# One order of issue replaced by another: the same 2916 pieces of DeltaNet attention and Fourier mixing, and 54 unread products on TensorE in place of 20

## The chip, the cores and the metric

The kernel runs on one core of a Trainium2 chip. The metric is the device time of one launch in microseconds (us). Five engines work from queues of their own, each in its own order: TensorE (PE, with its weight loads shown as PEld), VectorE (DVE), ScalarE (ACT), GpSimd (POOL) and SyncE (SP), which issues the DMAs. Everything is in float32.

## The reference

What must be computed, cut to what matters:

```
q, k, v: (4, 8, 768, 48)   beta: (4, 8, 768)   w_ch1: (384, 1536)   w_ch2: (1536, 384)

# attention (DeltaNet), for each batch and head, t = 0 .. 767
k_n   = k / (norm(k) + 1e-6);  state = 0                     # state is 48 x 48
y[t]  = q[t] @ state
state = state + beta[t] * outer(k_n[t], v[t] - state.T @ k_n[t])

x = y in the layout (batch, 768, 8 * 48 = 384)

# mixing, for each batch
u   = x + real(fft over the 384 channels of (fft over the 768 positions of x))
un  = (u - mean(u)) / sqrt(var(u) + 1e-6)                    # over the 384 channels
out = u + relu(un @ w_ch1) @ w_ch2
```

## The kernel before

**Attention.** The 768 positions of a batch are cut into six units (u0 to u5 for batch 0) of 128 positions, all 8 heads together. In a unit, the recurrence becomes products of 64x64 blocks and the inverse of a triangular matrix. Units are worked in rounds. The first round holds u0 and u1, the second u2 to u5, and both are prepared at once at the start of the kernel, which is called the **front** here. Its steps, with the names that the trace shows:

- `turn` transposes the keys on PE by products with a unit matrix (the helper line L358); ACT or DVE copies the result out of PSUM (L364 is a copy on ACT, L366 and L368 one on DVE).
- `keys` multiplies the transposed keys with each other (PE, 64x64 products; every ordinary matmul has the helper's line L355).
- `begin16` and `invert16` invert the 16x16 diagonal blocks on DVE, all heads at once, in pairs of a multiplication (L772) and an addition (L778) whose length changes from step to step. The steps of the two rounds alternate. Then come a scaling (L791) and two block transposes (L801 and L797).
- `join` puts the 16x16 inverses together to 32x32: DVE adds two of them (L832, into the tile `lo`), PE multiplies (`pp<-lo,w`), ACT copies the product back to `lo`, PE multiplies again (`pp<-lo,us`), and DVE subtracts the result in four pieces (L878) and transposes (L886, L887). After that come the 64x64 blocks, and the chain over the units.

Between these run the copies of `scale_v` (eight ACT copies of 128x48, `us<-us,nr`) and the decoding of weights (`f0` is L2019 and `f2` L2025 on ACT, then steps on DVE and POOL up to L2038).

**Mixing.** When a batch's attention is done, `seq6` does the transform over positions, and `feat` the one over channels: for each of six tiles T0 to T5 of 128 positions, PE writes two PSUM banks (`pp<-ft,R`), ACT copies the second of them to `ss`, and DVE adds and subtracts the first against it (L1530, L1533) and adds to `x` (L1537). `normed` normalises and `blockwise` transposes (L1591); a DMA through `zd` brings the transposed tile back as `R`. The MLP then runs in groups g0 to g2 of two tiles. For the last batch it is `mlpw`: a form with fewer products, in which DVE first adds and subtracts inputs (L1791) and weights (L1765), PE runs `first_w` (`pp<-R,w`, `pp<-us`, `pp<-us,w`, `pp<-R,us`) and `second`, and DVE takes the sums out of PSUM (L1962). The attention of batches 1 to 3 runs between the mixing of the batches before. The last batch's mixing, from about 512 us on, has no attention left beside it; this is called the **tail** here.

**What sets the order.** The program doesn't issue what it computes directly. `Plan.op` records 2916 pieces (one piece is what one engine does at one go: some matmuls, a copy, a DMA). `Plan.issue` then reads the text ORDER, 78 lines of signs, and issues the pieces in its order on all engines at once: two signs name a piece, one more the engine where a piece may run on one of several, one the PSUM bank for each bank that it opens, and two the piece after which a paced DMA may go. A number past the last piece calls `fill`:

```
            i = take(2)
            if i >= len(self.ops):
                fill(i - len(self.ops), take(1))
                continue
```

`fill(kind, bank)` issues products of the constant tile `pack` into a PSUM bank; nobody reads them. Kind 4 is one product of 128x128 by 128x256, which the trace shows as two passes under L2241; kind 3 is two products of 64x64 by 64x256 side by side; kind 0 is 18 small ones (L2235). A fill takes its place in PE's order as any other product, and it waits until what stood in its bank has been read out. Each engine works strictly in the order of ORDER, so that order also decides what stands behind a waiting instruction.

Of the kernel before, what the change touches and what calls it, by code (L numbers as in the profile page):

```python
# [62 lines left out]
CvDGtoAGrAnDeCDfDDgCiDjDiDhC0CHDCPGqCWDkDlDJABBXDmDKCGdC5CBGfC6CsDpAB1GeGgB4B5DqDoCBjC-DEDtCDrCDuCDs
CDnCCyB8B9CACBCECFCIASGyGyGlGzGfHCCTBZDACJDvFDwDxCDyCCMBkDLGHCNCQCRCUCVCYCZCcD0CCdCjBlDzCD3ABD5CCkD4
CClD1CDD6ED2CD8CDEOD7CFQEAECCEDCEBFAEEDHDdD9CEFCHMD+BCD-CEJEGETDG0CmEQCEKCFRCERBELCEUESCEPCEVCCnGnGo
EMEWDEXEYC7CVMKB1G6ETHEFUCENCEwEZEaEbEcEdFSCGpFTBEICEzCFVCFWDMG7CQGhEyCEfCGsGtFXCEHBEgDEhEkCElCEuFGE
vBDNCnFYAFZHfEYEiCEjCHOEeCDTELEmHHNEnFbFcDOBDQBHcEHHTHTFaEoCFdFeFfE2MmHEEpCErCDRBHPGuEqCG8G1E4BFhBEs
BCExAHDWDWE0FiGEtCHSHSE1CGvGwHQG3E5E+BCG2G4E7CE6BE8E3CE-CHeGhHGFjHdEfDPBFgCE9BGxG9FCFECHFHHHIFFCHVHP
FDDAFGFHBFlCFnCFmCFABCFLHUFZFkBFoHFNBFBBFpMnENHgHiHhFIMaEoFrCFMBHjHkFsCFJBNLFqCFOFPBHJFtCFuFGFKCDSE9
FyHWF0BMNGvMMFcFwBCIAE7FvCFzFHHRF1CHYF2MoGDG-HXG+HAMqCFxBH+FwF3BF7F9CF8CMLE6F4F5CHZHaHlF6BF+H0H0GACD  # L70
F-CGEMpCJNHyF9GBCGGCGCBCGHCHbMPF2GFGHH-G-GIIBF8GDCJMG5JOJPGKGJCMbMbHBHpFsJRJQGNGOBJTMcFDHoG+GMCH9GGH
8MpJSGLCGPCGQJVMdCJUJWJZGRCMeCJcMrABGUGWCGSCDDUFDJXMfEFGVCMtCGTBGXJYJaJbJeJfJiMOGPJdJgJjMgH1FNGYCHzF
zMhCJhHrGMJkGZCICJlJnJmJrDVG5JpJuHGH2MkCMwCMvCMjCH4H3MsJoJqHnFxJsHqJZMiCMuCH5H6JvJ3DCJ4HmMgJtMlJwQVM
hHsHtQ6MwHvHuHwH7MxJ1BJ5MyJMMRGOJxCJzCJ7CMzG5JyCJ0BIDM0EFJ9CJ6CHxKAABJ2CKJHDMQJoM2CM1BKBJ8CKDM-J7KSG
FKCJ-CJ+BKEKbCEKKKLKMIFKFKNIUJ5KTKcIEIGM+MiKGKkAEKUKVNABFKOKHKIKeNCCQXH2NBCIJIJKPKQM3GHKdIWJ1IVM0K2K
RKlK5KtFDKuK3BIHKWKXKYK6CIXM2INHsIIJkILJtNDDEIKJ0K4CK7CNJK8CIMHuQWJcM7CQiKlM6BIfKtIjK6KZIYKnNICM9NHC
KaKfKvKgKwQhKVRFM6IOIPNEQ5MeNFCM5BQRKTLHBM8CIeK6IiKSIgJ0NGCIQK+FIaIRISKhLRIZM4LSK9CIbIcQSNHLBDIhJ8Ki
NKLICLEEITNMK-CNNNONPIvKkIkIuNDIdNQNRNZNaNbNcNdLCCQjFGIsKKQlCQ7CHKjImLULFCIqIqLKBNeNfQ8CNgIlNhNiInIo
RGM3IrKYI5LHNjKmI4NGItKWIpNkI2NKLVJCQ8QkCNlNmQ9CNnNoNpNqNrNsNtQ+GHREQmDEQYKvQnIwIxIzKoLAFAI3QjZeLLCN
# [36 lines left out]
6e9BimBlTe+ilCXreLeMeNlUlVfAlWfCfDBjVi8Cffe-lXioFijDEeOfECfceTi+ABikCfBipfgeJjWFiqDEisCjDBlYlZlalbir
fJhYBjXCjCCitDjBClcldleeCi-EFivABiujYDfFjACjEEFeDfGfIfHiyfMjGBjZBXPjFePlflgfLjbCjcCfKjaClhlifNfOfQfR
fSfUljlkfhfafoDfTfXixCfpCllfiEjHDfjCfPizfWlmfVfqjdFCjeGHfrftjIjiCfkiwBjJDEflfmjhClnloeEjfCfsfnfuAHBl
plqfvCjKgegfClrfwCjgCf1jLClsjMDjyltlumPBmOBlvCeFgajOFEjNjjCDjzj0ktClwClxf2GjkjlClyDXtmQgbCjSjRmRElzB
j-lmjmCmSBf3CfzjnfxjQmTGfyf4f5f7mWBf0l0El1BjoCDgcmXBjPjqCf8f6l3BgDmVCjpl2BmUBj2l4Cl5GEmuCmtCmvkuBl9B  # L120
l8Cl+CggjrFjsl6DCl7Bf9Gf+Bl-CDmwFmxCmYGEmAmBCmCFmbCmcCmDf-mZCDmdCmEFGgAgEEj3maCmGBmFgFCghlwmHDgBj1mJ
CFj4mIgCgImyGm0BmeDEgGgHgJgKgLmgCmzCmMmfmNmKmLmhFm2CmijtCDm1BmjEFmkn9jugMgOgTgNgPkvBgQgRgSmlCgUgXn+g
VnKgdgdgijpn-oAnSGnUEnTBgWgYm3FAnVCm4HGjwm7CjvmmBnWmnoBoEm6CmoCEoCm5Cm9GHnLmqoDnbBm+mpmsncCoFmrnAFoH
nBoGoIoJnYm-CoKneCm8CnfCnXnCEFnECnZoNoMnaBGACoLnDnFHFoOngninhnjnInJjxnHnGoQoPoRoSoUoToWndnknlFnmCoXo
VnoHoYoZoagZnpCobocEDodnqokHFofCoeBnMnrohBojCj5oiBolomCopCo2EDo3oqBo4osFDoto5o6ovouo7o8owooBoxoyozo0
pAEDnnnNnto9orBnsonBo1poppBnupqnwproHo+ogCpBo-psptBpupDpCpEpFpKHFpLpNpMpOpUDFnOpPnynvpQpGnPnQn0pHpIp
# [2148 lines left out]
```

## Time and profile before

| What | Value |
| --- | --- |
| three runs | 628.64, 631.59, 635.98 us; median 631.59 |
| profiled execution | 629.09 us, of which the span of its instructions is 627.3 |
| mean granted TensorE clock in it | 0.985 |
| PE busy | 598.4 us (95% of the span) |
| DVE, ACT, POOL busy | 532.2 us (85%), 308.1 us (49%), 30.6 us (5%) |
| instructions | 22553 |
| moved by DMA | 40.65 MB, mean 65 GB/s |

The profile shows, for one execution, the busy time of each engine, the same in 40 slices of the span, the chain of work that ended last, and groups of instructions. PEclk is the TensorE clock that was granted, as a share of full speed. A PE row of the timeline joins matmuls of one kind that follow each other without a gap, and says in brackets how long PE was idle before and what ended that. A float32 matmul appears as two passes, except a transpose.

### The profile page before, as it was taken

The numbers are of one execution on the slowest core, as the hardware profiler recorded it, in microseconds if no ns is written. First come the engines' busy times: TensorE is split into PE (matmuls) and PEld (weight loads), VectorE is DVE, ScalarE is ACT, GpSimd is POOL, SyncE is SP. The second block draws the span as 40 slices with busy tenths as digits, with TensorE's granted clock in tenths as the row PEclk, the third lists the DMA queues.
The fourth block names the chain that finished last, engine by engine and source line by source line (L and its number), as shares of the span: only waits on it lengthen the run. The fifth ranks groups of instructions, "written<-read, shape, count | busy, mean of one in ns | idle before, by whom it ended". The sixth has DMA issues, their size and how long they took to land.

```text
span 627.3 us, 22553 instructions
## 1 busy us (share of the span) xinstructions
PE 598.4 (95%) x9674; PEld 520.5 (83%) x9674; DVE 532.2 (85%) x1460; ACT 308.1 (49%) x851; POOL 30.6 (5%) x39
## 2 busy tenths in 40 slices
PE   7789899989999989999999999999999998899997
PEld 6668798857778768799898878799989897899997
DVE  5978899999999879999889999998988987677464
ACT  5779777654447554856453256473433216233120
POOL 2001511230000000000000000000000000000000
PEclk9889999999999999999999999999999999799999
DMA  8625365432132421213113120503001001020101
GB/s 179 197 61 136 107 168 128 128 100 39 27 79 43 92 58 37 58 35 102 30 28 77 28 40 1 128 1 102 16 28 29 28 1 51 3 100 26 51 0 52
DMA packets 100578, 40.65 MB, mean 65 GB/s; under 512 B 88316, under 2 KB 95965, under 8 KB 100477
## 3 DMA queue, kind: packets, MB, share of 16 engines
q1 hardware_dynamic: 100285, 38.97, 24.3%
q8 instruction: 76, 1.25, 0.8%
q10 hardware_dynamic: 192, 0.23, 0.1%
q14 instruction: 25, 0.20, 0.1%
HBM read 30.14 MB, written 9.04 MB: 62 GB/s over the span
## 4 chain that ended last, share of the span: by engine, by line
PE 78%; DVE 12%; ACT 5%; issue 2%; DMA 1%; POOL 0%; DVEq 0%; SPq 0%; ACTq 0%; POOLq 0%
PE pp L355 75%; ACT us L364 2%; PE pp L358 2%; PE pp L2241 1%; DVE R L1377 1%; DVE x L1962 1%; DVE us L607 1%; DVE w L2038 1%; DVE pm L1377 1%; ACT R L364 1%; PE pp L2235 1%; DMA us<-in_q_dram 1%; DVE x L1352 1%; DVE u L1292 1%; DMA R<-in_k_dram 1%
## 5 line engine op out<-in xcount | busy, mean ns | idle before, releaser
L355 PE MATMUL pp<-R,w 128*128 128x256 f32 (+1 forms) x832 | 181.1, 368 | 0.0
L355 PEld LDWEIGHTS pp<-R,w 128*128 128x128 f32 x832 | 145.9, 192 | 18.7 <-issue 0.5
L355 PE MATMUL pp<-us 64*64 64x64 f32 (+6 forms) x2704 | 92.0, 236 | 12.0 <-ACT us L364 9.3
L355 PEld LDWEIGHTS pp<-us 64*64 64x64 f32 (+3 forms) x2704 | 76.9, 137 | 20.2 <-ACT us L364 12.9
L355 PE MATMUL pp<-w,R 128*128 128x384 f32 (+1 forms) x288 | 91.3, 441 | 1.8 <-DVE w L2038 1.8
L364 ACT ACTIVATE us<-pp 32x128 f32<-32x128 f32 (+4 forms) x149 | 57.9, 404 | 63.8 <-PE pp L355 39.3
L355 PEld LDWEIGHTS pp<-w,R 128*128 128x128 f32 x288 | 51.9, 190 | 24.4 <-DVE w L2038 2.4
L964 DVE TENSOR_TENSOR rr<-rr,tmp 128x30 f32<-128x30 f32 (+10 forms) x150 | 51.0, 340 | 3.1
L959 DVE TENSOR_TENSOR tmp<-rr 128x30 f32<-128x30 f32 (+10 forms) x150 | 48.9, 327 | 3.3
L1858 DVE TENSOR_TENSOR us<-us,pp 128x256 f32<-128x256 f32 x64 | 26.0, 419 | 18.5 <-ACT us L364 12.4
L355 PE MATMUL pp<-u,us 64*48 64x48 f32 (+2 forms) x1360 | 39.4, 216 | 0.2
L355 PEld LDWEIGHTS pp<-u,us 64*64 64x64 f32 (+1 forms) x1360 | 33.9, 130 | 5.8 <-issue 3.2
L1893 ACT ACTIVATE R<-pp 128x512 f32<-128x512 f32 x20 | 12.0, 598 | 40.0 <-PE pp L355 36.0
L364 ACT ACTIVATE gd<-pp 32x256 f32<-32x256 f32 x65 | 23.8, 374 | 15.4 <-PE pp L355 4.8
L355 PE MATMUL pp<-ft,R 97*128 97x97 f32 (+1 forms) x192 | 26.4, 283 | 4.6 <-DVE x L1962 3.7
L364 ACT ACTIVATE x<-pp 64x384 f32<-64x384 f32 (+2 forms) x39 | 17.0, 440 | 27.7 <-PE pp L355 13.3
L364 ACT ACTIVATE u<-pp 64x192 f32<-64x192 f32 (+1 forms) x65 | 21.2, 326 | 18.4 <-PE pp L355 10.8
L355 PEld LDWEIGHTS pp<-ft,R 97*128 97x128 f32 (+1 forms) x192 | 23.8, 193 | 6.6 <-DVE x L1962 3.8
L355 PE MATMUL pp<-R,ws 128*128 128x192 f32 x144 | 28.6, 329 | 0.1
L355 PE MATMUL pp<-us,gd 128*128 128x192 f32 x144 | 27.6, 326 | 0.0
L355 PE MATMUL pp<-st,us 48*64 48x48 f32 (+1 forms) x1104 | 25.7, 221 | 1.0 <-DVE u L366 0.5
L364 ACT ACTIVATE us<-us,nr 128x48 f32<-128x48 f32 x104 | 24.6, 322 | 2.4 <-DMA us<-in_v_dram 2.4
(217 smaller groups left out, 1082.9 us busy)
## 6 DMA issues: line engine op xcount, KB each, us to landing
R<-zd SPq DMA_DIRECT2D x44, 96.0 KB
out_dram<-x SPq DMA_DIRECT2D x11, 384.0 KB
us<-in_k_dram SPq DMA_DIRECT2D x16, 192.0 KB
us<-in_q_dram SPq DMA_DIRECT2D x16, 192.0 KB
us<-in_v_dram SPq DMA_DIRECT2D x16, 192.0 KB
x<-in_moe_w_ch_dram SPq DMA_DIRECT2D x11, 242.0 KB
zd<-tv SPq DMA_DIRECT2D x11, 192.0 KB
zd<-pm SPq DMA_DIRECT2D x11, 192.0 KB
```

Source lines behind the costliest of these rows:

```text
L355: I(nc.tensor.matmul(o, lhsT=lhsT, rhs=rhs, start=start, stop=stop, skip_group_check=True))
L358: I(nc.tensor.matmul(o, lhsT=src, rhs=ident[p0:p0 + n, p0:p0 + n], is_transpose=True, start=start, stop=True, skip_group_check=True))
L364: I(nc.scalar.activation(o, i, ACT.Copy, **({} if scale is None else {"scale": scale})))
L607: I(nc.vector.tensor_tensor(z.LT.rearrange(hs, s=2), span(b, 0, 128, [[64, NJ], [1, 64]]), m_su[:, None, None, :].broadcast_to([128, 2, NJ ...
L959: I(eng(e).tensor_tensor(T_, R[:, :, j + 1:32, j:j + 1].broadcast_to([128, ns, n, j]), R[:, :, j:j + 1, 0:j].broadcast_to([128, ns, n, j]) ...
L964: I(eng(e).tensor_tensor(R[:, :, j + 1:32, 0:j], R[:, :, j + 1:32, 0:j], T_, op=ALU.add))
L1292: I(nc.vector.tensor_tensor(U, U, span(b1, 64 * c, 64 * c + 64, [[D, m], [1, D]], s0), op=ALU.subtract))
L1352: I(nc.vector.tensor_tensor(w, w, v, op=ALU.add))
L1377: I(eng(e).tensor_tensor(o, i0, i1, op=op))
L1858: vec(256, lambda e: I(nc.vector.tensor_tensor(o, i0(), i1(), op=ALU.add)), [], [aH] + list(wr), pr - P.ev, use=n)
L1893: I(nc.scalar.activation(o, s, ACT.Relu))
L1962: vec(n, lambda e: I(nc.vector.tensor_tensor(o(), i0(), i1(), op=op)), rd, wr, pr - P.ev, use=use, due=due)
```

## The change

Only the text ORDER is replaced, by one that is a line longer, so that every line of the code below it has a number higher by one (L358 becomes L359, L2241 becomes L2242). The first line of each:

```diff
-ANBAPDAODALDAAADBAEDAMDAGDAHDACDAWAQDtkFAZANAYAaAHAbHAA6ANAXATABAKBAcCAeCBA7ANAdBAhFGAgBAfCAiAIDA4AN
+AMBAFDAYAAAPBAJDAWAEBACBtkAAZAPAKBAaAKAHDABAbFAAdBAIBAeGBAcCAhCDAgBAfCAiAUAAODAjATA6APBJHFA5AKA4A4A-
```

The 2916 pieces and their code are the same. What differs is their order on every engine; the engine of 190 pieces (91 go from DVE to ACT, 90 from ACT to DVE, 7 from POOL to DVE, 2 from DVE to POOL); the PSUM bank of nearly all; the piece that paces most DMAs; and the fills, of which there are 54 now (50 of kind 4, three of kind 3, one of kind 0) and were 20 (17, 2 and 1). They lie here:

| Place in the program | fills before | fills now |
| --- | --- | --- |
| front, up to the chain over u0 | 13, and kind 0 once | 34, and kind 0 once |
| later in the chain of batch 0 | 0 | 1 |
| middle, about 200 to 260 us | 6 | 8 |
| tail, between the `feat` tiles and ahead of the first `first_w` | 0 | 10 |

Two places in full; a row is a run of like instructions. First PE in the front, from the middle of the transposes to the second product of `join`. `us` here are keys, 128x64 rows are transposes, the 64x64 rows on `us` alone are `keys`, and `lo_74` is the tile `lo` of the first round. Before:

```order
L2241 MATMUL pp<-pack 128x256 x3
L358 MATMUL pp<-pack,us 128x64 x16
L2241 MATMUL pp<-pack 128x256 x3
L358 MATMUL pp<-pack,us 128x64 x24
L355 MATMUL pp<-us 64x64 x48
L355 MATMUL pp<-lo_74,w_65 64x64 x16
L2241 MATMUL pp<-pack 128x256
L355 MATMUL pp<-lo_74,us 64x64 x16
```

and with the change:

```order
L2242 MATMUL pp<-pack 128x256 x4
L359 MATMUL pp<-pack,us 128x64 x8
L2242 MATMUL pp<-pack 128x256 x3
L359 MATMUL pp<-pack,us 128x64 x8
L356 MATMUL pp<-us 64x64 x16
L359 MATMUL pp<-pack,us 128x64 x8
L2242 MATMUL pp<-pack 128x256 x2
L356 MATMUL pp<-us 64x64 x16
L2242 MATMUL pp<-pack 128x256 x2
L356 MATMUL pp<-us 64x64 x16
L356 MATMUL pp<-lo_74,w_65 64x64 x16
L2242 MATMUL pp<-pack 128x256
```

Fills now stand between single transposes and between the products of `keys`, up to the first product of `join`; before, none stood between the last transposes and `join`. (Ten more fills stand ahead of these rows now, seven of them in one row, where seven stood in one place before.)

On DVE at the same place, the last steps of `invert16` ahead of the addition L832 of the first round. Before:

```order
L772 TENSOR_TENSOR tmp<-w_66 128x52 x2
L778 TENSOR_TENSOR w_66<-w_66,tmp 128x2x13x2
L778 TENSOR_TENSOR w_66<-w_66,tmp 128x2x2x13
L772 TENSOR_TENSOR tmp<-w_66 128x72
L772 TENSOR_TENSOR tmp<-w_66 128x28
L778 TENSOR_TENSOR w_66<-w_66,tmp 128x2x12x3
L778 TENSOR_TENSOR w_66<-w_66,tmp 128x2x14
L791 TENSOR_TENSOR w_66<-w_66,gb 128x16x16 x2
L801 STREAM_TRANSPOSE rr<-w_66 128x16x32
L797 STREAM_TRANSPOSE gd<-w_66 128x16x32
L832 TENSOR_TENSOR lo_74<-gd,rr 128x128
```

and with the change:

```order
L773 TENSOR_TENSOR tmp<-w_66 128x52 x2
L779 TENSOR_TENSOR w_66<-w_66,tmp 128x2x2x13
L773 TENSOR_TENSOR tmp<-w_66 128x28
L753 STREAM_TRANSPOSE nr<-nr 128x32
L779 TENSOR_TENSOR w_66<-w_66,tmp 128x2x14
L792 TENSOR_TENSOR w_66<-w_66,gb 128x16x16 x2
L802 STREAM_TRANSPOSE rr<-w_66 128x16x32
L798 STREAM_TRANSPOSE gd<-w_66 128x16x32
L833 TENSOR_TENSOR lo_74<-gd,rr 128x128
L779 TENSOR_TENSOR w_66<-w_66,tmp 128x2x13x2
```

Three steps of the second round (an addition of 13x2 columns, and a pair of 72 columns) now come behind the addition to `lo`.

The second place is the tail. On PE, from the last products of the batch before (rows on `w_66`) to the first `first_w` (rows on `R_69`), with the `feat` rows on `ft,R_85` between. Before:

```order
L355 MATMUL pp<-w_66,us 128x192
L355 MATMUL pp<-ft,R_85 128x97
L355 MATMUL pp<-ft,R_85 128x96
L355 MATMUL pp<-ft,R_85 128x97
L355 MATMUL pp<-ft,R_85 128x96
L355 MATMUL pp<-R_69,w_65 128x128 x3
```

and with the change:

```order
L356 MATMUL pp<-w_66,us 128x192
L2242 MATMUL pp<-pack 128x256
L356 MATMUL pp<-ft,R_85 128x97
L356 MATMUL pp<-ft,R_85 128x96
L356 MATMUL pp<-ft,R_85 128x97
L356 MATMUL pp<-ft,R_85 128x96
L356 MATMUL pp<-ft,R_85 128x97
L356 MATMUL pp<-ft,R_85 128x96
L356 MATMUL pp<-ft,R_85 128x97
L356 MATMUL pp<-ft,R_85 128x96
L2242 MATMUL pp<-pack 128x256 x2
L2242 MATMUL pp<-pack 64x256 x2
```

Two tiles of `feat` instead of one stand behind the last sums of the batch before, and five fills (the last two in one more row) between T5 and `first_w`. T5's second bank, in both orders, is one of the four in which PE had gathered the sums of the MLP of the batch before: before, it was the one that DVE reads last (with an L1962), now it is the one that is read first.

On DVE at this place, from the L1533 and L1530 of a `feat` tile on. Before:

```order
L1765 TENSOR_TENSOR us<-w_65 128x384 x2
L1765 TENSOR_TENSOR us<-w_65,us 128x384
L1962 TENSOR_TENSOR x_83<-x_83,pp 128x192
L1765 TENSOR_TENSOR us<-w_65,us 128x384
L1962 TENSOR_TENSOR x_83<-x_83,pp 128x192
L1962 TENSOR_TENSOR u_71<-u_71,pp 128x192
```

and with the change:

```order
L1534 TENSOR_TENSOR eo_87<-pp,ss_93 128x191
L1531 TENSOR_TENSOR eo_87<-pp,ss_93 128x193
L1766 TENSOR_TENSOR us<-us,w_65 128x384
L1963 TENSOR_TENSOR x_83<-x_83,pp 128x192
L1963 TENSOR_TENSOR u_71<-u_71,pp 128x192
L1963 TENSOR_TENSOR x_83<-x_83,pp 128x192
L1531 TENSOR_TENSOR eo_87<-pp,ss_94 128x193
```

The reads of the old sums (L1963) now start behind one addition of weights (L1766); before, three such additions stood ahead of the first read and four ahead of the second. Two of the three reads shown empty, with an ACT copy, the bank that T5 now takes.

More of the change, by code (lines that the diff above doesn't have):

```diff
@@ L63 @@
[L63 to L67, printed above, removed]
@@ L123 @@
[L123 to L126, printed above, removed]
-VnRn3nzn1n2n4n5pWpXpJn7pRq+nxpeECpYpfpSpvpopwnGpxpypzq-Bp0pTp8DFn6p1GHp9rCrDCp+pZp2p-qAqBqQBDqRp3p4p
@@ new lines @@
+C1CCgANDCfDZCBWGyBHDFABDbCDXBtDcEDYCDdCiDGDaCDeCChtoFC0CDfEDgBwDiDjDJABtoFDKCDhDkDlBxDmB0GdB1CstoFB4
+C5ABDpFC6B5B8G0BkB9GmCyHCA+DqG7CvDoCDtCCACBCECFDrCG6BIDuCtoEtoDDsCC-CBDnCGlCICJBYDvEDACMDwCNDyCDxCDL
+HGCQBlDzCHLBxCRCUCVtoDCYCZtoDD0CD3AFHKCFD1DCBjDNDNCcGfGgCdD4CD5CD6ED2CD7CD8BCG8EAECCEDCEBDAD9CEED+BC
+EFCEJD-CGnGoCjClHMCkEOEGFQELCCnESCERCGrCRETFEICEPCDUDbFUBEQCEUEVCC7DqFRCHNG+FVCCmEWFEXGqDwEZEKCEaEYE
+bEcGsEdEMFSCGhFTBFWDMENCEwGuDHGfEeCEyCEgFDBFUFXCEfBGtEhEkCFYDHPEiCEuGHGpFZFdGvFaEjCElCEvCEmCEnHOHQGw
@@ new lines @@
+EzCE2FcFbEHBFeDPBEqCEpCEoCErCFgCEsBCDOBE4BNLExFAE0HEHUCcFhCG2EtBHSCnE+BCG1E1BE5G9E7CFfDSFZE6BG3G4HFF
+iHHTEME8E-CE3CE9CHVHMGxFjFlBDVEFHWFCFmCFEBFkCFDCDHHHdCdG-HAHcEeFFCHeNLHfGnMKGxFAGFH+H+FGFnCHXHYFoBFB
+BFHCFpFLG5HGHIFMCFtBFqCFNBFIFrBHgFsBDQBFOFuABHhIBGxMNFXHZHaHjFPCFyIAFHHiHkFvCF0CtoHMbFLF1CMMEgFzHAF2
+DRBF3CHBFwBCFxCFKCHbMnGpF7F8BF9BF4F6BFJCMmG9F+MaFDMoDGF5CJNMLE+MzF3DTEtHmF+GABCF-CMqCJMGCFGGEHJGBCHl
+GGBGFCBJOJPGHCGIGDCJQGJBMpCGKGNJTH-FtJUGMCGLCJRJVJSH8E2GOCGPCMcHAMdCGQGRCH0H0MrFGHpGCGUMeCJWJZJXJYJa
@@ new lines @@
+JbMuCHzG5GSDEGWCMfABHoGJGTBHnGPJeJfGVCGXJdMgHyFJJcMwCJgJkJjRSMhBJhGYCGZCMvCH1H1H2HrGHH9FFJ3HCJiJnJlJ
+qJmMjCJrJoJpJsH3JtMtCJuDEHqFwHsJvJwHtHvJ4HuHwMQHlDWJOMPFOH5H4H6MkCICMxJxBJzCJ5MlMyJZMsMRMRJyBMiCJ0BH
+xH7M+HsJ6CMOGPJ1BJ9CQ5GTIDJ-CKAFDKBKCKDJ2CJ+BKJEBJ7BQ6MtKKKMIXJrKSAGKEKLIEM-J0KTJ8CM0DCKFKGM1CNAGHIL
+J9KNKbBFKVKUKONCCM2CKHKIKcKPNBCK2KQKkHCKlKeKtEDK3GKRKdKuK5M3ABIWIWK4CKfIIKDKgIFIGQWMjKhIMJ9HRK6DNDFG
+KiK7CNGCNHCKWIUMiKXKmKnIHM8CNFCM5CLBDNICK8HNJIVGDIYIKJjQVKdM6BIaKYKZIZNEM7CQSJnIbIcKaLRLCCLECK9CNKIN
@@ new lines @@
+JcNMQhKeQiIHIjKDQRKUIeKLKjQjHDNNIdIJNFIOIiKVNONPQ7FGLFCKoIhJ+Q8CRFK4IPNQNRNZK+CQ9CNaNbNcIRIQISIgKZQk
+CQ+FGKwIfQ7KvLSM9QXH7LUNSNTI3LSI4QkQlCI2KGM4ITKxNdIkImRGIZQmDEQqBIuK6I5NZLHHNeNfNgRCCIlNhNiIrM9IqNgN
+jQoCInIoREK-CKyLVItQ+IpNkQYNdQrCI6IsNIIvNfIwIyJCQ+RBCQpCRDCI7I9NlNmNnNoQ-LICLABCNpNqQtKvNrZeJDIONsIx
+LKAIzI0JFK-NUNtKpLDQsLGJBK9LJNuI8I+I1RACNvJEM4NwNxJANjJGJHNyQUREKqLLCNzI-JIQnQTKaJJJKKzN0QuLKRHAHRJC
+QvDFQxBRICQwCLTNSLMN1KrJLMTLVN2QyFGKsQ1CQ2CRKDEN3N4RPCLNN5LWITLXNtASQ0BN6N7N8Q3CN9N+N-MUN9ROCQzRNCRM
@@ new lines @@
+CRROAQ4RTRURVRWRXRYOBOCODOEOFOGOHOIOJOKOLOMONOOOPOQORLYHK0LPLaALZCLcFHRgLbCOSOTOULdGMZOALfLgARhRiRjM
+VOJNWCLeCMSQwLiOVOWRLOXPyCOZBO0CO1BRkRlLjCRmOYCO2OaLhCK1RnRoRpLtLuO3GRqRQObALlRrLwLxNVCRsRtO4BPUCLkC
+RuRvO5COcCOdGOfCRwRxOgCLORyOhBMWKuPTCPVPzCLmEP0O6CRzO7CO8CO9CPWDOeCP1AMXQoP2COiBGOnCO+CAPXCOmCLoOlCP
+BCLyRQR0R1R2R3R4R5R6R7R8R9R+R-P3DLnCMYOgNYCPYGPCCPaCLQP6CLvLxOjBCOoEP5CPcCSASBSCSDSELzSAPDCQbK1LpPbC
+PZBOpOkCSFOqBCNXCLqSGO-EFPACPdGAPhCLrOrPiCPgBOtHOuOvEFRaSHPEGHSISJQZPZL2AOwCOsCPFPGCSKSLPHGSMSNSOPeB
@@ L134 @@
+3svsOsIs8GHs4s5sxswsKsMsNsys9s+s-tAtBszEADCs6tCtFs7tOHsPsSsQsRtDtEtPBtGtHtIGtJBtUtStKtLtNtQtRtTq9tMt
+VsTtZtatbtWtctdtetYthtjtXtftgti
 """
```

114 lines of the change are left out of this document (49 added, 65 removed).

## Prediction

> **What bounds the kernel now.** I read the page's busy times and slices first.
>
> ```profile
> span 627.3 us, 22553 instructions
> PE 598.4 (95%) x9674; PEld 520.5 (83%) x9674; DVE 532.2 (85%) x1460; ACT 308.1 (49%) x851; POOL 30.6 (5%) x39
> PEclk9889999999999999999999999999999999799999
> PE 78%; DVE 12%; ACT 5%; issue 2%; DMA 1%; POOL 0%; DVEq 0%; SPq 0%; ACTq 0%; POOLq 0%
> ```
>
> PE is the bound: busy for 95% of the span, 78% of the chain that ended last, and idle for only 627.3 - 598.4 = 28.9 us. An order can win back parts of that idle time, and the time that PE loses at a lower clock. The windows say where both lie (columns: length, then busy time of PE, PEld, DVE, ACT and POOL, then the granted clock).
>
> ```profile
> 0.00:25.00 25.00, 20.03 (x350) 16.45 (x350) 18.14 (x81) 14.71 (x38) 4.41 (x19) 0.93 0.80 186
> 25.00:50.00 25.00, 19.77 (x600) 17.19 (x603) 20.91 (x56) 19.63 (x55) 1.28 (x1) 0.86 0.36 96
> 50.00:75.00 25.00, 21.46 (x774) 19.62 (x772) 20.75 (x56) 21.32 (x50) 8.05 (x6) 1.00 0.49 135
> 84.00:520.00 436.00, 429.34 (x7012) 362.50 (x7004) 394.55 (x1064) 215.91 (x607) 13.88 (x11) 1.00 0.23 56
> 500.00:550.00 50.00, 45.50 (x333) 43.10 (x332) 38.74 (x101) 16.75 (x54) 0.00 (x0) 0.93 0.08 25
> ```
>
> The idle time is 13.7 us in the first three rows together (4.97 + 5.23 + 3.54) and 4.5 around the tail's start. The 436 us between hold 6.7, at full clock with PE 98% busy: there an order has little to win. The clock is below 1 in the front and around the tail (the 7 in the PEclk slices). Narrower windows show what precedes that.
>
> ```profile
> 9.00:12.00 3.00, 0.96 (x19) 0.75 (x18) 2.96 (x6) 2.04 (x6) 0.00 (x0) 1.00 0.68 159
> 15.00:18.00 3.00, 3.00 (x58) 2.61 (x51) 2.51 (x10) 1.28 (x3) 0.00 (x0) 0.50 1.04 304
> 27.00:30.00 3.00, 1.18 (x39) 1.17 (x40) 2.73 (x5) 3.00 (x9) 0.00 (x0) 0.76 0.89 305
> 30.00:33.00 3.00, 3.00 (x37) 2.23 (x35) 1.72 (x3) 1.83 (x9) 0.00 (x0) 0.50 0.04 12
> 57.00:60.00 3.00, 1.94 (x58) 1.66 (x54) 3.00 (x10) 2.89 (x8) 0.00 (x0) 1.00 0.37 103
> 532.00:540.00 8.00, 5.03 (x21) 4.86 (x22) 5.01 (x17) 1.62 (x6) 0.00 (x0) 0.61 0.00 0
> ```
>
> After 3 us with 0.96 or 1.18 busy the clock is halved a little later (0.50 at 15 to 18 and at 30 to 33); after 1.94 of 3 it isn't. In the tail it stands at 0.61 from 532 to 540. The fills are aimed at such places; whether they pay depends on what waits there. In the front that is the first `join`:
>
> ```profile
> 28.58 0.29 DVE L832 TENSOR_TENSOR lo<-gd,rr 128x128 f32<-128x128 f32 x1
> 28.83 1.02 PE L355 MATMUL pp<-us 48*64 48x64 f32 x27 [1.82 <-ACT us L364]
> 29.65 2.00 PE L355 MATMUL pp<-lo,w 64*64 64x64 f32 x31
> 31.57 1.22 PE L2241 MATMUL pp<-pack 128*128 128x256 f32 x2
> 31.68 0.28 ACT L364 ACTIVATE lo<-pp 128x128 f32<-128x128 f32 x1 [1.17 <-PE pp L355]
> 32.72 1.97 PE L355 MATMUL pp<-lo,us 64*64 64x64 f32 x32
> 34.81 0.28 DVE L878 SCALAR_TENSOR_TENSOR rr<-pp,pack,rr 128x64 f32<-128x64 f32 x1 [3.09 <-ACT w L364]
> 52.34 1.15 PE L355 MATMUL pp<-lo,w 64*64 64x64 f32 x32
> ```
>
> The same product takes 1.15 us at full clock, 2.00 here. DVE, which is nearly full until 28.6, idles 3.09 for the chain L832, PE, ACT, PE, L878. In the tail:
>
> ```profile
> 525.94 0.58 DVE L1591 STREAM_TRANSPOSE pm<-pm 128x384 f32<-128x384 f32 x1
> 534.97 1.17 PE L355 MATMUL pp<-ft,R 95*128 95x97 f32 x4 [3.67 <-DVE x L1962]
> 535.30 0.49 DVE L1791 TENSOR_TENSOR us<-R 128x128 f32<-128x128 f32 x2
> 535.93 2.39 PE L355 MATMUL pp<-R,w 128*128 128x128 f32 x8
> 540.25 1.65 PE L355 MATMUL pp<-R,w 128*128 128x128 f32 x10
> 542.85 1.49 PE L355 MATMUL pp<-R,w 128*128 128x128 f32 x10
> ```
>
> T5's second half waits 3.67 until an L1962 has read its bank, the clock falls, and the first `first_w` crawls. From there PE runs without a gap to the end, so what is won ahead of 535.93 is won for good.
>
> **What a fill costs.** At full clock and at the two lower speeds of the front:
>
> ```profile
> 609.11 5.34 PE L355 MATMUL pp<-R,w 128*128 128x256 f32 x24
> 16.35 4.60 PE L2241 MATMUL pp<-pack 128*128 128x256 f32 x16
> 12.42 1.16 PE L355 MATMUL pp<-us 48*64 48x64 f32 x62 [2.46 <-ACT us L364]
> 23.02 0.96 PE L358 MATMUL pp<-pack,us 64*128 64x64 f32 x24
> 31.86 1.90 ACT L364 ACTIVATE us<-us,nr 128x48 f32<-128x48 f32 x8
> 33.66 0.50 ACT L364 ACTIVATE w<-gd,pack 128x256 f32<-128x256 f32 x1
> 35.36 0.60 ACT L364 ACTIVATE us<-pp 128x512 f32<-128x512 f32 x1 [1.20 <-PE pp L358]
> 35.85 0.68 ACT L2025 ACTIVATE ws<-ws 128x512 int32<-128x512 uint32 x1
> 36.42 0.71 ACT L364 ACTIVATE us<-gd,pack 128x512 f32<-128x512 f32 x1
> ```
>
> A pass of 256 columns takes 5.34 / 24 = 0.222, so a fill of two passes 0.445; in the half-slow row 4.60 / 16 gives 0.575; wholly cold, 1.22 (the row at 31.57). The 34 fills more are 34 x 0.445 = 15.1 us of PE work, against 28.9 idle. They are free only where PE would have waited.
>
> **Front.** (1) DVE: three inversion steps of the second round move behind L832. By the last steps of the old trace's second round (72 and 28 columns),
>
> ```profile
> 44.55 0.23 DVE L778 TENSOR_TENSOR w<-w,tmp 128x72 f32<-128x72 f32 x1
> 45.53 0.19 DVE L778 TENSOR_TENSOR w<-w,tmp 128x28 f32<-128x28 f32 x1
> ```
>
> they are 0.2 to 0.23 each, so L832 comes about 0.6 earlier, at 28.0. (2) PE's own queue: 21 fills now stand between `join` and the place where the old fills of 16.35 begin: 21 x 0.445 = 9.3. The real work among them is 40 transposes at 0.96 / 24 and 48 products of `keys`, two passes each, at 1.16 / 62: 1.6 + 1.8 = 3.4. From 16.35 this ends at 29.05 with the clock up, a little earlier if PE comes there sooner. `join` has its input about 28.3 and starts between then and 29.5, so the fills eat most of the 0.6. (3) At full clock the first product takes 1.15 in place of 2.1 and ends at 29.5 to 30.7. (4) ACT now has one more `begin16` copy (0.50, the row at 33.66) ahead of the copy to `lo`; it was done 1.17 before that copy's 31.68, so it is ready at 31.0, and the copy runs there, 0.7 earlier. ACT sets this, which is why a start of `join` anywhere up to 29.8 costs nothing. (5) The fill between the products is then through, and the second product is warm: 31.3 to 32.5 in place of 34.7, and L878 comes 2.2 earlier. (6) ACT then has eight `scale_v` copies, an eviction and now two decode copies in place of one ahead of `us<-gd` (old start 36.42): 31.0 + 0.2 + 1.8 + 0.5 + 1.2 = 34.7. Net for the front **-1.7**. Ends: -3 if ACT isn't in the way, +0.5 if PE comes to `join` a microsecond late. The six fills behind it, at 0.445 each, lie in PE's waits for ACT up to 37; without that cover they cost 2.7.
>
> **Tail.** T5's second bank is now the one that is read first. Adding up DVE's pieces in the new order by their old durations, that bank is empty about 529 and T5 can go at 531, not 534.97 (an estimate: from the end of L1591 at 525.94 + 0.58 = 526.5, the seven pieces up to that read are 2.5). Then come five fills, 2.2, to about 533.2. From L1591 to L1791 DVE has 8.1 us of work, by old durations, in place of 8.8 (526.5 to 535.3), so `first_w` has its inputs about 534.5. It starts 1.4 earlier and warm: from 535.93 to 540.25 a set of 18 passes takes 4.32, the next one of 20, up to 542.85, 2.60, so 18 would take 2.3, a gain of 2.0. Net **-3.5**. Ends: 0 if the fills come 2 us late and take the place of the wait, -4.5 if `feat`'s earlier waits go too.
>
> **Middle.** Same pieces, both PE and DVE full, two fills more: +0.9 if nothing covers them, half of that if PE's 6.7 idle does: **+0.5**. Paces, banks and 190 changed engines can move it by ±3; the trace of before holds no row that prices them.
>
> Sum: -1.7 - 3.5 + 0.5 = **-4.7**, from 629.1 to 624.4 on the scale of the profiled execution. The three runs' median, 631.59, stands 2.5 above that one; from it the forecast would be 626.9. I take 626.
>
> [...]
>
> **Rivals.**
> - *Little is left* (0.22). ACT's extra copies hold `us<-gd` at 36, and the second round's inversion, which DVE ends at 45.5, gets back the three steps moved behind `join`; the tail gains half. For it: step (6) already takes back a quarter. -1.7: 630.
> - *Fills late in the queue, slower* (0.11). PE takes them in order, so a real product stands behind each. Should the clock stay low through them (as in 16.35), 21 cost 12.1 and the real work among them doubles to 6.8: from 16.35, `join` starts near 35 and not at 29.54, +5.5; five tail fills at 1.22 end after T5 plus 6, so nothing is won there; +1 for the cold rest. 636 to 639. It decides from the point where the last fill ends over 1.5 us after L832. Against it: five fills instead of two now stand ahead of the wait of 2.46 and take the window 9 to 12 from 0.96 to about 2.3 busy (three more at 0.445).
> - *More* (0.15). PE's 8.8 idle us from 25 to 75, which later rounds' waits make, shrink as well, the second `join` comes earlier, `feat` loses its waits. -10: 620.
> - *The clock doesn't hold* (0.07): fills wait for their banks as the work does, leave the windows as empty, and only the earlier DVE order counts, -0.6 and -1.4: 629.
>
> **How the numbers follow.** The forecast has 0.45, with its own range 622 to 630. No more than 1% (6.3 us) can be told from no change by three runs that spread over 7.3. Below 625.3: two fifths of the forecast's cases, nearly all of "more", a little of the others: 0.40. Above 637.9: most of "slower" and stray cases of the middle: 0.10. The range reaches from "more" less 2 to the near side of "slower": 618 to 634.
>
> **What would show it.** Right: PEclk 1.0 throughout 15 to 36; `pp<-lo,w` and `pp<-lo,us` near 1.15 each; L878 near 32.6; the wait of 3.67 ahead of T5 gone or under 1; the first `first_w` about 2.5 long and starting 3 to 5 before the old 535.93, the front's gain included; PE busy about 608. Wrong: `join` starting after 30.5 with fills right ahead of it; 84 to 520 longer than 439; a new idle row ahead of the first sums of `mlpw`; the fills showing waits of their own.

## The result and the profile after

| | before | with the change |
| --- | --- | --- |
| median of 20 runs each, side by side | 631.18 us | 625.07 us |
| ratio of the runs, 95% interval | | 0.9921 [0.9899, 0.9943] |
| profiled execution, span | 629.09, 627.3 us | 624.12, 622.3 us |
| mean granted clock in it | 0.985 | 0.999 |

Predicted were 626 us, and on the scale of the profiled execution 4.7 less than before; the spans differ by 5.0. Medians, here and below, count all executions of a kernel and ratios leave out the few slow ones (1176 and 2057 us among them); without those no median moves by more than 0.3.

The page after, span, busy times and clock:

```profile
span 622.3 us, 22736 instructions
PE 608.8 (98%) x9744; PEld 527.7 (85%) x9744; DVE 533.3 (86%) x1464; ACT 311.4 (50%) x866; POOL 30.8 (5%) x34
PEclk9999999999999999999999999999999999999999
```

PE is busy for 10.4 us more, though the real work is the same: the 34 fills more bring some 15 by the prediction's price, and the 5 that are missing fit the products that now run at full clock. Its idle time is 13.5 us where it was 28.9. Four of the windows of before, now:

```profile
0.00:25.00 25.00, 23.60 (x364) 19.55 (x367) 18.80 (x83) 15.42 (x36) 3.48 (x14) 1.00 0.84 199
25.00:50.00 25.00, 22.83 (x661) 19.28 (x662) 23.76 (x63) 20.72 (x60) 2.89 (x2) 1.00 0.41 109
84.00:520.00 436.00, 432.07 (x6981) 365.73 (x6970) 391.72 (x1064) 222.89 (x631) 13.15 (x11) 1.00 0.22 54
500.00:550.00 50.00, 49.84 (x354) 46.21 (x352) 38.88 (x101) 20.67 (x67) 0.00 (x0) 1.00 0.13 39
```

Most of the idle time is gone in the front and in the tail, and the clock is 1.00 in both. The front in the timeline (PE, ACT, DVE):

```profile
27.63 1.13 PE L2242 MATMUL pp<-pack 128*128 128x256 f32 x4
28.70 0.69 PE L356 MATMUL pp<-us 48*64 48x64 f32 x32
29.21 1.10 PE L356 MATMUL pp<-lo,w 64*64 64x64 f32 x32
30.24 0.70 PE L2242 MATMUL pp<-pack 128*128 128x256 f32 x2
30.87 1.15 PE L356 MATMUL pp<-lo,us 64*64 64x64 f32 x32
30.36 0.28 ACT L365 ACTIVATE lo<-pp 128x128 f32<-128x128 f32 x1 [0.30 <-PE pp L356]
34.09 0.71 ACT L365 ACTIVATE us<-gd,pack 128x512 f32<-128x512 f32 x1
28.11 0.29 DVE L833 TENSOR_TENSOR lo<-gd,rr 128x128 f32<-128x128 f32 x1
32.15 0.28 DVE L879 SCALAR_TENSOR_TENSOR gd<-pp,pack,gd 128x64 f32<-128x64 f32 x1 [0.68 <-PE pp L356]
```

`lo` is ready at 28.4 and `join` starts at 29.21, behind two fills and a product of its own queue: there the fills cost 0.8. Both products run warm, and the subtraction stands at 32.15 instead of 34.81. The tail:

```profile
528.74 1.92 PE L356 MATMUL pp<-ft,R 97*128 97x97 f32 x16
530.50 2.70 PE L2242 MATMUL pp<-pack 128*128 128x256 f32 x12
533.03 1.26 PE L356 MATMUL pp<-R,w 128*128 128x128 f32 x8
535.25 1.49 PE L356 MATMUL pp<-R,w 128*128 128x128 f32 x10
```

T4 and T5 run without a wait, five fills follow, and the first set of `first_w` takes 2.22 (533.03 to 535.25), not 4.32. Setting the starts of PE's pieces against before: 2.5 us earlier at 48, 1.4 at 82, 3.1 at 150, mostly between 1 and 4 up to 500, 3.2 at the last batch's `seq6` (509.78, before 512.94), 2.9 at the start of `first_w`, 5.0 at the end.

### The profile page after: what moved, and what is told of

Read it like the earlier page. It is cut to its first block, busy times and chain, and to the rows that moved or that the text cites. A ratio compares the mean times of both kernels' runs of the same rounds, so it can differ in the third digit from the quotient of the medians.

```text
span 622.3 us, 22736 instructions
## 1 busy us (share of the span) xinstructions
PE 608.8 (98%) x9744; PEld 527.7 (85%) x9744; DVE 533.3 (86%) x1464; ACT 311.4 (50%) x866; POOL 30.8 (5%) x34
## 3 DMA queue, kind: packets, MB, share of 16 engines
q8 instruction: 76, 1.25, 0.8%
## 4 chain that ended last, share of the span: by engine, by line
PE 49%; ACT 1%; DVE 1%; issue 0%; DVEq 0%
PE pp L356 47%; PE pp L2242 1%; DVE x L1963 0%; PE pp L359 0%; ACT us L365 0%; ACT R L365 0%; ACT x L365 0%; ACT gd L365 0%; DVE u L1963 0%; DVE u L1293 0%; ACT mv L1559 0%; DVE t L995 0%; DVE us L369 0%; ACT u L365 0%; DVE ws L1815 0%
## 5 line engine op out<-in xcount | busy, mean ns | idle before, releaser
L356 PE MATMUL pp<-us 64*64 64x64 f32 (+5 forms) x2704 | 88.5, 233 | 2.2 <-DVE us L629 0.6
L356 PEld LDWEIGHTS pp<-us 64*64 64x64 f32 (+3 forms) x2704 | 74.3, 134 | 10.4 <-issue 3.6
L965 DVE TENSOR_TENSOR rr<-rr,tmp 128x30 f32<-128x30 f32 (+10 forms) x150 | 48.9, 328 | 3.2
L1894 ACT ACTIVATE R<-pp 128x512 f32<-128x512 f32 x22 | 13.1, 597 | 44.4 <-PE pp L356 40.9
L365 ACT ACTIVATE u<-pp 64x192 f32<-64x192 f32 (+1 forms) x56 | 18.1, 325 | 32.8 <-PE pp L356 30.1
L365 ACT ACTIVATE x<-pp 64x384 f32<-64x384 f32 (+2 forms) x45 | 18.9, 432 | 25.1 <-DVE u L1293 14.8
L2242 PE MATMUL pp<-pack 128*128 128x256 f32 (+1 forms) x112 | 29.9, 403 | 0.0
L1670 ACT ACTIVATE R<-pp 128x512 f32<-128x512 f32 x24 | 14.1, 592 | 26.4 <-PE pp L356 23.4
```

The source lines that it names most:

```text
L356: I(nc.tensor.matmul(o, lhsT=lhsT, rhs=rhs, start=start, stop=stop, skip_group_check=True))
L365: I(nc.scalar.activation(o, i, ACT.Copy, **({} if scale is None else {"scale": scale})))
L965: I(eng(e).tensor_tensor(R[:, :, j + 1:32, 0:j], R[:, :, j + 1:32, 0:j], T_, op=ALU.add))
L1670: I(nc.scalar.activation(o, s, ACT.Relu))
L1894: I(nc.scalar.activation(o, s, ACT.Relu))
L2242: I(nc.tensor.matmul(pst[x, 512 * bank:512 * bank + 256], lhsT=w[x, 0:128 // tiles], rhs=w[x, 0:256], start=True, stop=True, skip_group_ch ...
```

## The experiments

Each kernel is the one before or the changed one with a small edit. In the diffs, `nth` counts the fills in the order of issue (0 to 53 in the changed kernel: 1 to 34 in the front, 44 to 53 in the tail); `ADD` names fills (kind, bank) that are issued ahead of a piece.

**The changed kernel without the later fills of the front.**

```diff
+    DROP = range(14, 35)
-                fill(i - len(self.ops), take(1))
+                (fill if next(nth) not in self.DROP else min)(i - len(self.ops), take(1))
```

> The changed kernel without 21 of its 34 fills in the front, those from the last transposes on (13 are left, as many as before the change). Theory (the fills hold the clock up to join): the clock falls to about 0.5 near 27 to 33 as before the change, lo,w and lo,us take about 2.0 each instead of 1.1, and the first L879 stands at 33.8 to 34.8 instead of 32.15; the span is 1.5 to 2.5 longer than the changed kernel's 622.3. Rival (the new order of DVE and ACT gives the front's gain, the fills nothing): L879 at 32.5 or earlier, the span unchanged or shorter by up to 0.5.

Median 628.75 (624.06 to 631.63 in 12 runs), ratio to before 0.9968 [0.9936, 1.0000]. The profiled execution is the fastest one, with a span of 622.3 as in the changed kernel:

```profile
26.25 1.99 PE L356 MATMUL pp<-us 48*64 48x64 f32 x64 [0.46 <-ACT us L365]
28.44 1.85 PE L356 MATMUL pp<-lo,w 64*64 64x64 f32 x32 [0.21 <-DVE lo L833]
30.67 1.15 PE L356 MATMUL pp<-lo,us 64*64 64x64 f32 x32 [0.38 <-ACT lo L365]
31.95 0.28 DVE L879 SCALAR_TENSOR_TENSOR gd<-pp,pack,gd 128x64 f32<-128x64 f32 x1 [0.82 <-PE pp L356]
```

The clock fell as expected (0.50 granted from 24 to 30), and the first product takes 1.85. But nothing stands in the queue ahead of it: it starts at 28.44, ends at 30.3 as with the fills, and the second finds the clock back. L879 is even 0.2 earlier. In this execution the fills are worth nothing, as the rival said. The twelve runs say otherwise: their clocks go from 0.977 (631.63) to 0.995 (624.06), those of the changed kernel from 0.991 to 1.000. How much of `join` falls into the slow stretch differs from run to run, as one more trace shows: the kernel without both sets of fills (further down) has the same front, and in its execution of 631.49 both products were slow.

```profile
31.15 1.97 PE L356 MATMUL pp<-lo,us 64*64 64x64 f32 x32 [0.38 <-ACT lo L365]
33.24 0.28 DVE L879 SCALAR_TENSOR_TENSOR gd<-pp,pack,gd 128x64 f32<-128x64 f32 x1 [1.77 <-PE pp L356]
```

There L879 comes 1.3 later than in the execution above. With the fills the granted clock was 1.00 from 24 to 36, in the trace after and in that of the kernel without the tail's fills. Both theories expected the same of every execution, and neither was right.

**The changed kernel without the fills of the tail** (`DROP = range(44, 54)`, the edit otherwise as above).

> The changed kernel without its 10 fills in the tail. Theory of the prediction (two parts: T5's bank is free early, which brings first_w's start forward by about 1.4 to 3 whatever the fills do; the fills keep the clock): first_w starts within 0.5 of 533.0, the wait ahead of it is 2 to 3 us, the clock falls, and its first 18 passes take 3.5 to 4.3 instead of 2.2; span +1.5 to +2.2. Rival (the order alone gives the whole tail gain): 18 passes in 2.2 to 2.5 and the span within 0.3 of 622.3.

Median 624.24, ratio 0.9915 [0.9882, 0.9949], span 622.4: as with them.

```profile
525.89 1.92 PE L356 MATMUL pp<-ft,R 97*128 97x97 f32 x16
530.18 2.50 PE L356 MATMUL pp<-R,w 128*128 128x128 f32 x8 [2.37 <-ACT ss L365]
534.61 2.23 PE L356 MATMUL pp<-R,w 128*128 128x128 f32 x10
```

T4 and T5 come at 525.89 instead of 528.74, `first_w` starts 2.85 earlier, and then takes 4.43 for its first set instead of 2.22; the set after it starts slow as well (2.23 for ten passes instead of 1.49) and loses another 0.7. The amounts cancel. The expectation of a start at 533.0 missed: the fills ahead of T5 held up the `feat` tiles, and through them ACT and DVE.

**The kernel before with seven fills in its front, and with seven in its tail.** Two kernels; each has one of the two `ADD` lines.

```diff
+    ADD = {171: ((4, 4),) * 3, 197: ((4, 2),) * 4}     # front
+    ADD = {2654: ((4, 4),) * 7}                        # tail
-            o, self.ins = self.ops[i], None
+            o, self.ins = self.ops[i], [fill(*f) for f in self.ADD.get(i, ())] and None
```

> The kernel before with seven fills more, all in the tail, in T5's first bank ahead of T5, inside its wait of 3.67; nothing else is moved. Theory: T5's second half still starts at 534.97 on this trace's scale and first_w at about 535.5, but warm: its first 18 passes in 2.2 to 2.4 instead of 4.3, span 2.0 to 2.7 shorter than 627.3. Rival (the bank and the order of DVE are what counted): span within 0.5 of 627.3, the passes still at 3.5 or more.

The tail: median 628.57 against 630.48, ratio 0.9976 [0.9938, 1.0014], so by time alone not told from no change; by the trace it is clear.

```profile
532.73 3.19 PE L2241 MATMUL pp<-pack 128*128 128x256 f32 x14
536.98 0.69 PE L355 MATMUL pp<-ft,R 95*128 95x97 f32 x4 [0.65 <-DVE x L1962]
537.50 1.29 PE L355 MATMUL pp<-R,w 128*128 128x128 f32 x8
539.75 1.49 PE L355 MATMUL pp<-R,w 128*128 128x128 f32 x10
```

This execution was 2.0 later than before when it came to the tail (T5's second half at 536.98, before 534.97). The fills lie inside the old wait, and the first set takes 2.25 instead of 4.32; piece by piece the 2.0 are made up and 0.7 more are won by its end. Seven fills inside a wait that stays are worth 2.7 in this trace.

> The kernel before with seven fills more, all in the front: three ahead of the gram products of u0 and four ahead of those of u4, where PE waited 1.61 and 1.82; nothing else is moved. Theory (the clock is worth about 2 us at join, whatever the rest of the order): clock 1.0 through 27 to 36, lo,w and lo,us near 1.15 each, first L878 at 32.2 to 32.8 instead of 34.81; of that 1 to 2.5 is left in the span (624.8 to 626.3 beside 627.3). Rival (the gain needs the new order of DVE and ACT): L878 above 34, the span within 0.5 of 627.3.

> The kernel before with seven fills in the front, once more for its trace, since its first profile fell into an execution at half speed throughout. The five ordinary executions were 636 to 641, where I had expected 625 to 626. Theory 1 (the fills delay a transfer or an eviction that later work waits for): a new wait of 5 us or more between 30 and 140, with join itself warm. Theory 2 (the fills wait themselves for their banks and hold back gram): fills that start after 28, join later than 31. Theory 3 (a matter of that chip): this time 625 to 628.

The front, twice: 638.04, ratio 1.0130 [1.0079, 1.0181], then 635.76, ratio 1.0096 [1.0061, 1.0131]. Slower, where both sides had expected a gain or nothing.

```profile
28.54 1.99 PE L2241 MATMUL pp<-pack 128*128 128x256 f32 x8
30.19 0.29 DVE L832 TENSOR_TENSOR lo<-gd,rr 128x128 f32<-128x128 f32 x1
30.98 1.10 PE L355 MATMUL pp<-lo,w 64*64 64x64 f32 x32
32.64 1.15 PE L355 MATMUL pp<-lo,us 64*64 64x64 f32 x32
33.90 0.28 DVE L878 SCALAR_TENSOR_TENSOR rr<-pp,pack,rr 128x64 f32<-128x64 f32 x1 [0.64 <-issue]
```

`join` is warm and L878 comes at 33.90, 0.9 earlier, though this execution was 1.6 late at 21 us, ahead of the first added fill. Then PE loses time in jumps: 1.3 at 87, 0.9 at 185, 1.8 at 189, 1.9 at 437 and smaller ones, some 10 us up to 490. It isn't the chip (the two sets ran on different ones), and no engine is waited for: each jump stands at a wait that the profile can't put down to anything. Behind the longest of these, with PE busy for only 2.29 of the 4 us from 440, the granted clock was 0.60 from 444 to 448, which cost another 1.7. What the traces show of these waits stands under the last heading. In sum, count and longest, of before, of this kernel and of the next one:

```profile
PE pp L355 <- issue: 2.4, 3, 1.2
PE pp L355 <- issue: 6.9, 9, 1.7
PE pp L355 <- issue: 1.5, 3, 1.0
```

**The same fills, with as many of PE's instructions ahead of the rest as before.**

```diff
-            for i in range(6 * OPEN):
+            for i in range(6 * OPEN - 7):
```

> The kernel before with the seven fills in the front as in b_front2, and seven of the 18 small unread products at the very start left out, so that the number of PE's instructions ahead of everything after join is as before the change. In b_front2 join was 0.9 earlier, but PE then lost 10 us between 85 and 490 in jumps of 0.9 to 2, several of them with PE waiting for nothing that the profile shows. Theory (the jumps come from the places at which PE's instructions are fetched, and these moved with the number of instructions): the jumps are gone, span 624.5 to 626.5, median 627 to 629. Rival (the fills in the front cost this in another way): median 634 to 638 again.

Median 629.31 against 631.94, ratio 0.9949 [0.9914, 0.9984]; the third row above is its. At 35 us it stands 0.1 ahead of before, at 186 us 0.2, with a jump of -1.2 at 65 between that later goes back, and 0.1 behind at `seq6`; the 10 us are gone, as the theory said. The span is 627.3, where 624.5 to 626.5 was expected: this execution is 2.65 late at 21 us, ahead of the first added fill (the kernel with the fills alone was 1.6 late there, so about 1 of it may be the price of the seven products that are missing at the start), and `join` makes that up. From L832 to L878 it takes 3.7 in both kernels with the fills (30.19 to 33.90, and 31.22 to 34.94) and took 6.2 before (28.58 to 34.81). So seven fills ahead of `join` are worth 2.5 in both traces.

**The changed kernel with the same seven products fewer at the start, and nothing else.**

> The changed kernel with seven of the 18 small unread products at the very start left out and nothing else changed: PE waits there for the first transfer. Theory (places of the fetches count): front to 48 as in the changed kernel within 0.5, then PE's waits without a cause lie at other places and add to something else; the median differs from 625 by 2 us or more, up or down. Rival: median within 1 of 625, waits at the same places.

Median 628.13, ratio 0.9945 [0.9909, 0.9981], so 3 us are lost. But the theory is not borne out: the waits without a cause lie at other places, as it said, but sum to 1.5 (three), and the loss is nearly all in the first 11 us (3.4 of 3.7 in this trace). The start of this kernel, and the same fills in the changed one:

```profile
5.00 1.32 PE L359 MATMUL pp<-pack,us 64*128 64x64 f32 x16 [1.07 <-DMA us<-in_k_dram]
9.99 4.63 PE L2242 MATMUL pp<-pack 128*128 128x256 f32 x10
```

```profile
8.81 2.43 PE L2242 MATMUL pp<-pack 128*128 128x256 f32 x10
```

PE was idle for 1.07 ahead of the first transposes; afterwards five fills take 4.63 instead of 2.43, with the next transposes behind them. So seven of the 18 products at the start, unread as well, were worth 2.2 us at these fills alone in this trace (4.63 - 2.43).

**The changed kernel with two GpSimd additions elsewhere.** The trace after shows two L792 that take 1.5 each where they took 0.4 before, just ahead of the second round's `join`; GpSimd works at L2036 meanwhile. The edit moves four pieces in the text ORDER, `Gf`, `Gg`, `Gn` and `Go` (two L2031 of DVE, two L2036 of GpSimd), to behind `FQ`, the second L833 of that round.

> The changed kernel with four pieces of the decoding (two L2031 on DVE and the two GpSimd additions L2036 behind them) moved behind the second round's L833. In the changed kernel these additions run at 42.5 to 45.4, beside two L792, which take 1.5 each instead of 0.42. Theory (a GpSimd addition holds up a DVE instruction with two inputs in SBUF): L792 x2 back to 0.76 in all, the second round's L833 at 44.4 to 45.2 instead of 47.7, PE's wait of 1.28 for it gone, the span 0.5 to 1.5 shorter. Rival (chance, or a wait of another kind): L792 as long as before, L833 only 0.8 earlier, which is the two pieces that went behind it.

DVE and GpSimd in the changed kernel, then in this one:

```profile
42.72 2.96 DVE L792 TENSOR_TENSOR w<-w,gb 128x256 f32<-128x256 f32 x2
42.51 1.44 POOL L2036 TENSOR_TENSOR w<-w,ws 128x512 int32<-128x512 int32 x1 [38.50 <-DVE w L779]
43.91 1.49 POOL L2036 TENSOR_TENSOR w<-w,x 128x512 int32<-128x512 int32 x1
47.69 0.49 DVE L833 TENSOR_TENSOR lo<-gd,rr 128x128 f32<-128x128 f32 x2
```

```profile
41.85 0.76 DVE L792 TENSOR_TENSOR w<-w,gb 128x256 f32<-128x256 f32 x2
44.67 0.49 DVE L833 TENSOR_TENSOR lo<-gd,rr 128x128 f32<-128x128 f32 x2
45.64 1.36 POOL L2036 TENSOR_TENSOR w<-w,ws 128x512 int32<-128x512 int32 x1 [41.64 <-DMA us<-in_v_dram]
48.27 0.81 PE L356 MATMUL pp<-lo,w 64*64 64x64 f32 x20 [1.47 <-issue]
```

With the additions moved, L792 is back to 0.76, and L833 comes at 44.67 instead of 47.69, of which 2.2 are the two L792 and 0.8 the two L2031 that now come behind it. The time didn't follow: median 625.78 beside 624.97, ratio 0.9932 [0.9901, 0.9963], span 623.9. PE takes up `join` earlier, and then waits without a cause, 1.47 in the middle of the first product, and at 61.19, 65.68, 70.30, 74.85 and 78.95 again. The sums for the changed kernel and for this one:

```profile
PE pp L356 <- issue: 1.9, 5, 0.7
PE pp L356 <- issue: 6.2, 9, 1.5
```

**The changed kernel without both sets of fills, and the changed kernel itself beside it.**

> The changed kernel itself, as it stands, so that the next three have its runs on the same chip: median 623 to 626, a granted clock of 0.99 to 1.0 in every run, and runs that spread by less than those of the kernel before.

> The changed kernel without the 21 later fills of the front and without the 10 of the tail: its order with fewer fills (23) than pieces of it stand in the order before plus three. Theory after the first four runs (order and fills each give a part; the front's fills count in most executions, the tail's not at all): median 2.5 to 4.5 above that of the changed kernel beside it, clock 0.98 to 0.99, wide spread; first_w starts near 530 and its first pieces are slow. Rival 1 (the order gives all, the fills nothing): median within 1 of the changed kernel. Rival 2 (the fills give all): median within 1 of the kernel before.

The changed kernel: 624.97 (623.67 to 626.32 in 6 runs), ratio 0.9920 [0.9892, 0.9948]. Without the 31 fills: 627.37 (623.67 to 631.49 in 12 runs), ratio 0.9938 [0.9910, 0.9967], clocks of 0.975 to 0.992. The difference of 2.4 lies just below what the theory said (2.5 to 4.5), and the intervals overlap. The order, with 23 fills in place of 20, is clear of no change; that the 31 fills add to it is likely from these two kernels and the runs without the front's fills, not certain. What in the order gives its part was not taken apart: no run here restores a piece of the old order.

**The changed kernel with only the last five fills of the tail** (`DROP = range(44, 49)`).

> The changed kernel without the first five of its ten fills in the tail (those ahead of T5); the five between T5 and first_w stay. Theory (a fill ahead of a piece on the path costs its length, one behind the last such piece only keeps the clock): first_w starts at 530.1 to 530.5 as without any fills in the tail, but warm, 18 passes in 2.2 to 2.4; the span 2.0 to 2.8 shorter than the changed kernel's 622.3, the median 622 to 623.5. Rival (too little PE work in the 3 us before, the clock falls all the same): 18 passes in 3.5 or more, the median within 1 of 625.

> The kernel of a_tail5 once more, on a fresh set of runs, because its first set held only five ordinary executions and its profile fell on one in which PE had lost 1.7 more than the changed kernel at 61 us without a cause. Theory: median 621.5 to 624, ratio to the kernel before 0.985 to 0.990, first_w warm and 1 to 3 earlier than in the changed kernel. Rival (the first set was luck): median 624.5 to 626, as the changed kernel.

Median 623.28, ratio 0.9841 [0.9795, 0.9887], and once more 623.41, ratio 0.9854 [0.9813, 0.9894], against 0.9921 of the change. The first set's profile:

```profile
527.60 1.92 PE L356 MATMUL pp<-ft,R 97*128 97x97 f32 x16
529.36 2.70 PE L2242 MATMUL pp<-pack 128*128 128x256 f32 x12
531.89 1.37 PE L356 MATMUL pp<-R,w 128*128 128x128 f32 x8
534.21 1.49 PE L356 MATMUL pp<-R,w 128*128 128x128 f32 x10
```

From T4 to `first_w` it takes 4.29, as without any fill (525.89 to 530.18), and `first_w` is warm (2.32). This execution was 1.9 later than the changed kernel at 483, for PE lost 2.0 between 57 and 63 at two waits without a cause, and it is 1.1 earlier at `first_w`. The spans are 621.3 and 623.1, so the medians are the evidence: 1.6 us better than the change, the best version here. Both intervals end just below where that of the change in the result begins (0.9899); the smaller set of the changed kernel above, on another chip, begins at 0.9892.

## Why the prediction was right, point by point

- *The sum*: that 4.7 and 5.0 agree so well is luck. The front gave 2.5 where 1.7 was forecast, the middle 0.7 where a loss of 0.5 was, and the tail only 1.8 where 3.5 was; these errors, of 0.8, 1.2 and 1.7, cancel. What held was where the time lay and in which direction each place would go, apart from the middle.
- *Front (1), L832 at 28.0*: 28.11. *(2), `join` between 28.3 and 29.5*: 29.21, behind its fills; without them 28.44, so the fills eat 0.8. (The rows there that the text ahead of the prediction calls `keys` are the `gram` products of the queries, and the transposes theirs; the counts and times are the same.) *(3)*: 1.10. *(4), ACT sets the copy at 31.0*: wrong by 0.6. The copy ran at 30.36 and waited 0.30 for PE; so PE set it, and the fills ahead of `join` weren't quite free. *(5), L878 at 32.6*: 32.15. *(6), `us<-gd` at 34.7*: 34.09. The front gave 2.3 there and 2.5 at 48, not 1.7.
- What the fills of the front are for wasn't seen rightly: they were to hold the clock in every execution, but one trace without them loses nothing, another loses 1.3, and the gain is in the runs' spread. The sum compared two executions; by the medians, which come from different chips in part and whose intervals overlap, these fills are worth some 2 to 4 us.
- *Second round*: no step looked at GpSimd. Its two additions took 2.2 from DVE, and the front's gain at the second L833 was 1.0.
- *Tail, -3.5*: the term was mis-sized. From `seq6` to the end 1.8 were won. The warm `first_w` is as worked out (2.1 against 2.0). The start, 1.4 earlier, failed: relative to `seq6`, `first_w` starts 0.3 later than before (and 2.9 before the old 535.93, where the sign of being right was 3 to 5). The bank came free as read from the order (no wait at T5), and `first_w` could have started at 530.18, but the five fills ahead of T5 put all of it 2.85 back. The prediction counted only the five behind T5; its rival of late fills had the mechanism, and the tail was its place.
- *Middle, +0.5 within 3*: -0.7 in this pair of traces. One known part is a wait for a decoded weight, 1.8 at 139 before (L2038), which is gone. Edits that leave the order of the middle as it is moved it by up to +10 (the kernel before with seven fills in its front), by waits without a cause and a fallen clock; the bound of 3 was too narrow.
- *The clock*: the prediction read a halving behind 3 us with 0.96 or 1.18 busy, where PE's longest waits were 2.46 and 1.82. Without the front's fills the clock fell as well, and no wait of PE was longer than 2.56 there: behind waits of 2.56 and 1.62, with 0.46 busy between them (19.39 to 24.03), the granted clock was 0.50 from 24 to 30. In the kernel with fewer products at the start, five fills ran at half pace in a window whose granted clock is given as 1.00 (the third number from the end); there the durations show it, not the column:

```profile
9.00:12.00 3.00, 3.00 (x22) 2.52 (x22) 2.84 (x4) 2.27 (x5) 0.00 (x0) 1.00 0.88 232
```

## What to carry to other kernels

In these runs a filler product was free only behind the last piece that something waits for (five there left the way from T4 to `first_w` at 4.29 us, as without any): put it between that and the wait's end, as long as the wait. Ahead of such a piece the fills cost 0.8 us at `join` and 2.85 at T5, and the clock that they hold has to pay for that. Judge what holds a clock by many executions, since one trace can fall on a lucky one. And when a small edit moves the time in places that it doesn't touch, count PE's waits without a cause, and see where they stand among its instructions, before looking for a reason nearby.

## What the runs showed of the hardware

- Beside two GpSimd additions of 128x512 int32 (1.44 and 1.49 us), two L792 took 2.96 together, and 0.76 when the additions were moved: 2.2 us for the pair. That it takes two inputs in SBUF, as the expectation has it, is not shown: beside the moved additions an L2023, which has one, took 1.51 (from 47.00) where another took 0.42 (at 53.44). Nor was every instruction with two held up: in the trace after, an L2039 at 62.62 took 0.68 beside an addition that itself took 1.96.
- By the traces, PE's waits without a cause are waits for its own instructions. The profile's page counts 76 packets on a queue for instructions, 1.25 MB, so 16 kB each. The traces hold 19457 to 19605 instructions of PE (products and weight loads, and 109 and 117 others in the traces before and after), so one packet comes to about 256 of them (19457 / 76). The thirteen traces of ordinary length have 57 such waits, 0.2 to 1.75 long, and all of them stand at one place of that count: the instruction that comes late is number 193 or 194 behind a multiple of 256. It starts 1.1 to 1.65 us after the packet that is due there has landed; in the kernel with the moved additions, the wait ends at 48.27 and its packet landed at 46.77, and the waits from 61.19 to 78.95 are 256 instructions apart (within one), 4.1 to 4.6 us. Seven fills are 28 instructions (19485 instead of 19457), so other pieces came to stand at these places. Why a wait stands at some of these places and not at others is not shown: a trace has 2 to 9 such waits, and the kernel with the moved additions has nine where the changed one, with the same instructions of PE in the same order, has five. Most of the 76 packets show no wait, but the waits at the others sum to up to 6.9 us in one execution (nine in the kernel before with seven fills in its front).
- The kernel before took longer in runs with a lower granted clock: 627.25 at 0.988 and 635.25 at 0.972 within one set of 26 runs.
